# Products of the identity in TensorE's three waits ahead of the first FFN unit

## The chip, the cores and the metric

The kernel runs on one core of a Trainium2 chip. The metric is the device time of one execution in microseconds (us). TensorE (PE in the profile) multiplies, ScalarE (ACT) evaluates functions and copies, VectorE (DVE) does elementwise work and reductions, GpSimd (POOL) one elementwise step per pair of tiles, and SyncE (SP) issues the DMAs. Each engine takes its instructions in program order, and engines wait for each other by semaphores.

## The reference

Two stages. First, attention within chunks of 64 rows, for 8 batches, 8 heads, 576 rows and 64 columns per head:

```python
scores = scale * np.matmul(q_c, k_c.transpose(0, 1, 2, 4, 3))
attn = np.exp(scores - np.max(scores, axis=-1, keepdims=True))
attn = attn / (np.sum(attn, axis=-1, keepdims=True) + 1e-09)
out = np.matmul(attn, v_c)
```

Its output, laid out as 4608 tokens by 512, then goes through a feed-forward block with weights of 512 x 2048 and 2048 x 512:

```python
h = x @ w_in
g = h * (1.0 / (1.0 + np.exp(-1.702 * h)))
return (g @ w_out).astype(np.float32)
```

The weights arrive as 8-byte floats, which the kernel turns into pairs of 4-byte ones itself.

## The kernel before

The 4608 tokens are 36 tiles of 128, in 9 groups of 4. For each group the FFN is done in 16 units; unit j holds 128 columns of `w_in` and the matching 128 rows of `w_out`. Every large product is made of three products of fp32r parts (high by low, high by high, low by high), lines 634 to 636 for h, lines 669 to 671 for the output; the very first unit does h in two halves of 256 tokens (lines 647 to 649), the second of which needs tiles 2 and 3.

The first four tiles have code of their own, `plan_first(u)` for u = 0 to 3. For one tile: transposes of q and k (`t_pe`, L266), copies, scores (`s_pe`, L289), maximum and subtraction (DVE, L294 and L295), exponential (ACT, L298), sum and reciprocal (DVE, L302 to L305), normalisation (POOL, L308), transposes of the probabilities (`e_pe`, L313, tile eTp), their copy (`e_act`, ACT, L320), the product with v (`x_pe`, L329, tile x), and the split of its result in a high part (`x_hi`, ACT, L339) and a low part (`x_lo`, DVE, L342). The transposes of probabilities go to PSUM bank po2 for even u and po3 for odd u.

Over the same microseconds ACT and DVE convert the weights, `plan_w(j)`: ACT L172 and L176, DVE L181 and L182, DVE L188 (join), ACT L193 (high part of the unit's weights), DVE L196 (low part). FFN unit j needs both parts. After h of a unit, ACT applies the function and copies the high part (L655, L656), DVE makes the low part (L660, tile g_l), and only then may L669 begin.

The order of instructions on every engine is written once by `Plan.emit`: each step has an engine, a cost, a rank and what it needs, and a list scheduler with these costs picks the order. What a step's function emits has no influence on that order; only the step's cost and rank have.

Ahead of everything stands a warm-up: 7 products of the 128 x 128 fp32 identity with itself, in PSUM bank po3, planned at 3.4 us.

Of the kernel before, what the change touches and what calls it, by code (L numbers as in the profile page):

```python
# [9 lines left out]
F32 = mybir.dt.float32  # L10
# [8 lines left out]
PE, ACT, DVE, POOL, DMA = "pe", "act", "dve", "pool", "dma"  # L19
# [79 lines left out]
def tile_chunk_attention_ffn(  # L99
# [9 lines left out]
    nc = tc.nc  # L109
# [4 lines left out]
    P = 128  # L114
# [11 lines left out]
    WARM = 7  # L126
# [5 lines left out]
    ps_o = ctx.enter_context(tc.tile_pool(name="ps_o", bufs=1, space=bass.MemoryType.PSUM))  # L132
# [3 lines left out]
    ident = const.tile([P, P], F32, tag="ident", name="ident")  # L136
# [6 lines left out]
    plan = Plan(buffers)  # L143
# [9 lines left out]
    def plan_w(j):  # L153
# [58 lines left out]
        plan.add(ACT, 1.05, rank - 3.5, part_h, need=[e("wj")], make=e("wh"))  # L212
        plan.add(DVE, 1.25, rank - 2, part_l, need=[e("wh")], make=e("w"), give=["tmp"])


    x_h, x_l = {}, {}

# [23 lines left out]
    def plan_first(u):  # L241
# [68 lines left out]
        def e_pe():  # L310
            st["ps"] = ps = ps_o.tile([P, NP, 2, CH], F32, tag=f"po{2 + u % 2}", name=f"eTp_{u}")
            for n in range(NP):
                nc.tensor.transpose(  # L313
                    ps[:, n].rearrange("p h i -> p (h i)"),
                    st["e"][:, n].rearrange("p c j -> p (c j)"),
                    ident,
                )

        def e_act():
            nc.scalar.activation(st["et"], st["ps"], AF.Copy)  # L320

        def x_pe():
            va, et = st["v"], st["et"]
            ps = ps_a.tile([P, 2, 2, NP, CH], F32, tag="att", name=f"x_{u}")
            for n in range(NP):
                for h in range(2):
                    for c in range(2):
                        r = slice(64 * c, 64 * c + 64)
                        nc.tensor.matmul(  # L329
                            ps[64 * h : 64 * h + 64, c, 0, n, :],  # L330
                            va[r, 2 * n + h, :],
                            et[r, n, h, :],
                            start=True,
                            stop=True,
                        )
            st["x"] = ps[:, :, 0].rearrange("p c n i -> p n c i")

        def x_hi():
            nc.scalar.activation(x_part(x_h, u), st["x"], AF.Copy)  # L339

        def x_lo():
# [14 lines left out]
        plan.add(DVE, 1.1, rank + 0.6, s_sum, need=[ev("ex")], make=ev("z"))  # L356
        plan.add(POOL, 1.07, rank + 0.6, s_norm, need=[ev("z")], make=ev("n"))
        plan.add(PE, 0.5, rank + 1.7, e_pe, need=[ev("n")], make=ev("ep"), take=[f"po{2 + u % 2}"])
        plan.add(ACT, 0.6, rank + 1.7, e_act, need=[ev("ep")], make=ev("et"), give=[f"po{2 + u % 2}"])
        plan.add(  # L360
            PE, 0.75, rank + 1.5, x_pe, need=[ev("et"), ev("v"), "xa_0"], make=ev("xp"),
            take=["att", "att"], give=[slot(1)],
        )
# [354 lines left out]
                    make=f"st_{n}_{t}", give=[tag],  # L718
                )

    def warm_up():

        ps = ps_o.tile([P, P], F32, tag="po3", name="warm")
        for _ in range(WARM):
            nc.tensor.matmul(ps, ident, ident, start=True, stop=True)

    plan.add(PE, 3.4, -1000, warm_up)
    for u in range(TB):
        plan_first(u)
    for u in range(TB, NTL, 2):  # L730
# [41 lines left out]
```

## Time and profile before

| | us |
|---|---|
| median of 3 runs | 868.29 |
| lowest, highest | 868.08, 869.13 |
| the profiled execution | 868.24 |
| its span, first to last instruction | 866.5 |
| time outside the span (868.24 - 866.5) | 1.7 |
| PE busy | 849.3 |
| DVE busy | 392.3 |
| ACT busy | 319.1 |

The page gives averages over a long steady stretch, some 820 us, in which TensorE works without a pause. The part around the change is the ramp ahead of it, between about 21 and 41 us from the span's start, and is to be read from views cut to that stretch: the order of time on single engines, the busy time of short windows, and the chain that ended last. Start times in the order of time are relative to the span's start. TensorE's rows have a record for each pass that the profiler saw, and one matmul instruction of the program may leave more than one record: the 7 products of the warm-up are 14 records.

### The profile page before, as it was taken

Reading aid. Unit: us, or ns where it says so; the run is one execution under the profiler, and the core shown is the slowest. Engines: PE = TensorE matmul, PEld = TensorE weight load, DVE = VectorE, ACT = ScalarE, POOL = GpSimd, SP = SyncE. Lnnn points to the kernel's source line nnn. Section 1 sums busy time; section 2 is a strip of 40 time slices with the busy share of each in tenths; the row PEclk is TensorE's granted clock in tenths of the full one; section 3 lists DMA queues with packets and bytes.
Section 4 is the critical chain, followed back from the end, with each engine's and each line's share of the span. In section 5 each row is a group of like instructions: output and inputs, shape, how many; then the busy total and the mean of one; then the engine's idle time right before and its main releaser. Section 6 shows DMA issues by size and latency. Waiting matters only on the chain.

```text
span 866.5 us, 14153 instructions
## 1 busy us (share of the span) xinstructions
PE 849.3 (98%) x5882; PEld 703.0 (81%) x5882; DVE 392.3 (45%) x511; ACT 319.1 (37%) x459; POOL 32.3 (4%) x24
## 2 busy tenths in 40 slices
PE   7699999999999999999999999999999999999998
PEld 5588888888888888888888888888888888888886
DVE  5899985353534252616253444445343524121111
ACT  3999652332424242324242423223241424222221
POOL 1000000000000000000000000000000000000000
PEclk9799999999999999999999999999999999999999
DMA  9997243234313022402231232113101010010001
GB/s 236 319 300 212 45 74 80 52 56 73 92 25 49 22 47 57 72 2 48 74 58 18 41 75 51 31 38 85 25 1 26 37 35 3 1 45 5 1 0 49
DMA packets 194592, 55.47 MB, mean 64 GB/s; under 512 B 179680, under 2 KB 187872, under 8 KB 194528
## 3 DMA queue, kind: packets, MB, share of 16 engines
q1 hardware_dynamic: 194528, 54.57, 27.3%
q8 instruction: 46, 0.75, 0.4%
q14 instruction: 18, 0.15, 0.1%
HBM read 45.09 MB, written 9.44 MB: 63 GB/s over the span
## 4 chain that ended last, share of the span: by engine, by line
PE 95%; SPq 2%; DMA 1%; DVE 1%; ACT 1%; issue 1%; POOL 0%; DVEq 0%; POOLq 0%; ACTq 0%
PE po L669 16%; PE po L670 15%; PE po L671 15%; PE hp L634 15%; PE hp L635 15%; PE hp L636 15%; PE s L445 2%; PE x L510 2%; SPq L231 1%; DMA raw<-in_moe_w_out_dram 1%; PE qkTp L412 0%; ACT raw L172 0%; POOL first_b L308 0%; PE eTp L480 0%; SPq L163 0%
## 5 line engine op out<-in xcount | busy, mean ns | idle before, releaser
L660 DVE TENSOR_TENSOR g_l<-hp,g_h 128x512 fp32r<-128x512 f32 x144 | 99.5, 691 | 351.2 <-ACT g_h L656 350.1
L669 PE MATMUL po<-w,g_l 128*128 128x512 f32 x576 | 226.4, 393 | 0.1
L671 PE MATMUL po<-w,g_h 128*128 128x512 f32 x576 | 224.3, 389 | 0.0
L670 PE MATMUL po<-w,g_h 128*128 128x512 f32 x576 | 224.2, 389 | 0.0
L634 PE MATMUL hp<-x_l,w 128*128 128x512 f32 x572 | 223.2, 390 | 0.0
L636 PE MATMUL hp<-x_h,w 128*128 128x512 f32 x572 | 222.7, 389 | 0.0
L635 PE MATMUL hp<-x_h,w 128*128 128x512 f32 x572 | 222.6, 389 | 0.0
L655 ACT ACTIVATE hp<-hp 128x512 f32<-128x512 f32 x144 | 83.9, 583 | 305.3 <-PE hp L636 269.6
L656 ACT ACTIVATE g_h<-hp 128x512 fp32r<-128x512 f32 x144 | 86.1, 598 | 141.3 <-PE po L671 139.6
L669 PEld LDWEIGHTS po<-w,g_l 128*128 128x128 f32 x576 | 108.1, 188 | 23.9 <-DVE g_l L660 1.0
L671 PEld LDWEIGHTS po<-w,g_h 128*128 128x128 f32 x576 | 108.1, 188 | 22.7
L670 PEld LDWEIGHTS po<-w,g_h 128*128 128x128 f32 x576 | 108.1, 188 | 21.8
L636 PEld LDWEIGHTS hp<-x_h,w 128*128 128x128 f32 x572 | 107.4, 188 | 22.8 <-DVE w L196 0.4
L634 PEld LDWEIGHTS hp<-x_l,w 128*128 128x128 f32 x572 | 107.4, 188 | 22.4 <-DVE g_l L660 0.2
L635 PEld LDWEIGHTS hp<-x_h,w 128*128 128x128 f32 x572 | 107.4, 188 | 22.0
L493 DVE STREAM_TRANSPOSE eT<-e 32x512 f32<-32x512 f32 x112 | 78.7, 703 | 29.6 <-POOL e L473 27.8
L473 POOL TENSOR_TENSOR e<-e,r 128x1024 f32<-128x1024 f32 x14 | 26.7, 1905 | 671.8 <-ACT hp L655 671.8
L427 DVE STREAM_TRANSPOSE qkT<-raw 128x1024 f32<-128x1024 f32 x28 | 34.7, 1240 | 29.4 <-PE s L445 26.8
L525 ACT ACTIVATE x_h<-x 128x512 fp32r<-128x512 f32 x32 | 17.4, 593 | 58.4 <-PE x L510 58.4
L466 DVE TENSOR_REDUCE z<-e 128x16 f32<-128x1024 f32 x16 | 19.5, 1219 | 22.2 <-ACT e L462 22.2
L528 DVE TENSOR_TENSOR x_l<-x,x_h 128x512 fp32r<-128x512 f32 x32 | 20.6, 685 | 6.7 <-ACT x_h L525 6.7
L445 PEld LDWEIGHTS s<-qkT 64*64 64x64 f32 x1024 | 18.2, 135 | 5.6 <-issue 5.3
(64 smaller groups left out, 410.5 us busy)
## 6 DMA issues: line engine op xcount, KB each, us to landing
out_dram<-ob SPq DMA_DIRECT2D x36, 256.0 KB, 2.0
raw<-in_moe_w_in_dram SPq DMA_DIRECT2D x16, 512.0 KB, 7.8
raw<-in_moe_w_out_dram SPq DMA_DIRECT2D x16, 512.0 KB, 8.3
v<-in_v_dram SPq DMA_DIRECT2D x28, 256.0 KB, 3.3
raw<-in_q_dram SPq DMA_DIRECT2D x144, 32.0 KB, 2.0
raw<-in_k_dram SPq DMA_DIRECT2D x144, 32.0 KB, 2.0
raw<-in_q_dram SPq DMA_DIRECT2D x48, 24.0 KB, 1.9
raw<-in_k_dram SPq DMA_DIRECT2D x48, 24.0 KB, 1.9
```

What stands on the lines that cost most here:

```text
L427: nc.vector.transpose(st["tr"][:, i].rearrange("p n (t j) -> p (n t) j", j=32), st["raw"][:, i].rearrange("p n t j -> p (n t) j"),)
L445: nc.tensor.matmul(o, tr[r, 0, n, cols], tr[r, 1, n, cols], start=True, stop=True)
L493: nc.vector.transpose(st["et"][po : po + 32, :, 32 * a : 32 * a + 32], st["e"][pi : pi + 32, :, 32 * b : 32 * b + 32],)
L634: nc.tensor.matmul(hp, wh, xl, start=cc == 0, stop=False)
L635: nc.tensor.matmul(hp, wh, xh, start=False, stop=False)
L636: nc.tensor.matmul(hp, wl, xh, start=False, stop=cc == NCC - 1)
L655: nc.scalar.activation(h_t[g], h_t[g], AF.Gelu_apprx_sigmoid)
L656: nc.scalar.activation(gh, h_t[g], AF.Copy)
L660: nc.vector.tensor_tensor(gl, h_t.pop(g), gh.bitcast(F32), op=ALU.subtract)
L669: nc.tensor.matmul(po, gl[:, c], w[:, 0, :], start=j == 0, stop=False)
L670: nc.tensor.matmul(po, gh[:, c], w[:, 0, :], start=False, stop=False)
L671: nc.tensor.matmul(po, gh[:, c], w[:, 1, :], start=False, stop=j == NF - 1)
```

## The change

The warm-up's function becomes `keep_warm(count, bank)`, and it is called at three more places, inside steps that exist: 36 products into po3 right behind the transposes of tile 2's probabilities, 15 into po3 right behind tile 2's product with v, and 4 into po2 right behind the transposes of tile 3's probabilities. No result of these products is read. Costs and ranks of the steps stay as they were, also of the two steps that grew.

```diff
+    def keep_warm(count, bank):
+
+        ps = ps_o.tile([P, P], F32, tag=bank, name="warm")
+        for _ in range(count):
+            nc.tensor.matmul(ps, ident, ident, start=True, stop=True)
+
...
                     st["e"][:, n].rearrange("p c j -> p (c j)"),
                     ident,
                 )
+            if u == 2:
+                keep_warm(36, "po3")
+            if u == 3:
+                keep_warm(4, "po2")
...
             st["x"] = ps[:, :, 0].rearrange("p c n i -> p n c i")
+            if u == 2:
+                keep_warm(15, "po3")
...
-    def warm_up():
-
-        ps = ps_o.tile([P, P], F32, tag="po3", name="warm")
-        for _ in range(WARM):
-            nc.tensor.matmul(ps, ident, ident, start=True, stop=True)
-
-    plan.add(PE, 3.4, -1000, warm_up)
+    plan.add(PE, 3.4, -1000, lambda: keep_warm(WARM, "po3"))
```

TensorE's order before, from tile 2's transposes of probabilities to the first FFN unit. Numbers in names only tell buffers apart: eTp_320 and x_340 belong to tile 2, eTp_364 and x_379 to tile 3, hp_401 is h of the first unit.

```order
L313 MATMUL eTp_320<-ident,first_b_150 128x128 x4
L329 MATMUL x_340<-first_b_150 64x64 x16
L313 MATMUL eTp_364<-ident,first_b_197 128x128 x4
L329 MATMUL x_379<-first_b_197 64x64 x16
L647 MATMUL hp_401<-x_l_81,w_369 128x256
```

The same place in the changed kernel, whose lines stand 6 to 12 further down. The x of tile 2 is now x_377, tile 3's transposes are eTp_417, its x is x_437.

```order
L319 MATMUL eTp_320<-ident,first_b_150 128x128 x4
L219 MATMUL warm<-ident 128x128 x36
L339 MATMUL x_377<-first_b_150 64x64 x16
L219 MATMUL warm<-ident 128x128 x15
L319 MATMUL eTp_417<-ident,first_b_197 128x128 x4
L219 MATMUL warm<-ident 128x128 x4
L339 MATMUL x_437<-first_b_197 64x64 x16
L659 MATMUL hp_459<-x_l_81,w_427 128x256
```

Nothing changed places; three runs of products were put in, each ahead of an instruction that waits for another engine. In the program tile 3's transposes now wait for TensorE's own 15 products too, whose bank po3 they write.

ScalarE's order over the same stretch, in the changed kernel: the high parts of tiles 2 and 3 (x_h) and the copy of tile 3's probabilities (first_b_197<-eTp_417) stand between steps of the weights' conversion.

```order
L172 ACTIVATE raw_245<-raw_245 128x1024
L351 ACTIVATE x_h_80<-x_377 128x4x128
L176 ACTIVATE raw_245<-raw_245 128x1024
L193 ACTIVATE w_427<-wtmp_365 128x1024
L330 ACTIVATE first_b_197<-eTp_417 128x512
L172 ACTIVATE raw_305<-raw_305 128x1024
L351 ACTIVATE x_h_80<-x_437 128x4x128
L176 ACTIVATE raw_305<-raw_305 128x1024
```

On ScalarE, VectorE, GpSimd and the DMA queue the order is the same as before, but for buffer numbers and line numbers.

## The prediction

> **What bounds the kernel now.** I began with the page's busy shares, went to short windows around the change, then to the chain that ended last, and last to the single engines in order of time. The page first:
>
> ```profile
> PE 849.3 (98%) x5882; PEld 703.0 (81%) x5882; DVE 392.3 (45%) x511; ACT 319.1 (37%) x459; POOL 32.3 (4%) x24
> PEclk9799999999999999999999999999999999999999
> ```
>
> TensorE is busy 98% of the span, and the granted clock falls in one slice near the start (the 7). Five windows show where:
>
> ```profile
> core 0: us, PE busy (x) PEld busy (x) DVE busy (x) ACT busy (x) POOL busy (x), PEclk, DMA share, GB/s
> 21.74:25.16 3.42, 0.00 (x0) 0.00 (x0) 1.27 (x2) 2.43 (x3) 0.00 (x0) 1.00 1.07 379
> 25.16:28.57 3.41, 1.13 (x32) 0.94 (x32) 3.27 (x7) 3.19 (x5) 1.50 (x1) 0.50 1.06 381
> 31.98:35.40 3.42, 3.42 (x16) 3.42 (x17) 3.38 (x4) 3.42 (x4) 0.00 (x0) 0.50 1.05 158
> 35.40:40.56 5.16, 5.03 (x31) 3.80 (x29) 4.91 (x7) 5.10 (x8) 0.00 (x0) 1.00 1.08 287
> ...
> 40.56:862.60 822.04, 822.04 (x5520) 680.03 (x5520) 363.63 (x469) 294.21 (x427) 26.67 (x14) 1.00 0.23 53
> ```
>
> TensorE does nothing for 3.42 us, then has half the clock from 25.16 to 35.40. From 40.56 to 862.60 it is never idle, and the view of its waits has no row after 41 us. So whatever the change does before 40.56 arrives at the end as it is: the time moves by as much as the first output product (L669 at 40.56) moves. And from 25 to 40.56 ACT and DVE are nearly full too (5.10 and 4.91 of 5.16 us in the fourth window). The chain of waits, in order of time, says who sets 40.56:
>
> ```profile
> 22.73 1.11 ACT raw L172
> 23.86 0.71 DVE wtmp L181
> ...
> 27.07 1.86 POOL first_b L308
> ...
> 34.70 0.95 ACT w L193
> ...
> 39.82 0.70 DVE g_l L660
> ...
> 40.56 0.50 PE po L669
> ```
>
> It goes through the weights' conversion on ACT and DVE; TensorE's small steps of tiles 2 and 3 hang between. So TensorE's half clock is paid mostly beside a queue that is full anyway, but a late TensorE step stops that queue, since ACT takes its instructions in order.
>
> **The cost of one fill product.** The trace has such products only in the warm-up, at half clock. TensorE's rows in order of time, and two sources:
>
> ```profile
> 1.36 3.35 PE L725 MATMUL warm<-ident 128*128 128x128 f32 x14 [1.36 <-POOL ident masks.py:199]
> ...
> 16.78 1.04 PE L266 MATMUL qkTp<-ident,first_a 128*128 128x128 f32 x8
> 17.75 0.69 PE L329 MATMUL x<-first_b 64*64 64x64 f32 x32
> ...
> 21.06 0.65 PE L313 MATMUL eTp<-ident,first_b 128*128 128x128 f32 x4 [1.22 <-POOL first_b L308]
> 25.91 1.13 PE L329 MATMUL x<-first_b 64*64 64x64 f32 x32 [4.19 <-ACT first_b L320]
> 28.97 1.12 PE L313 MATMUL eTp<-ident,first_b 128*128 128x128 f32 x4 [1.93 <-POOL first_b L308]
> 30.78 1.13 PE L329 MATMUL x<-first_b 64*64 64x64 f32 x32 [0.69 <-ACT first_b L320]
> ...
> 35.66 0.28 PE L647 MATMUL hp<-x_l,w 128*128 128x256 f32 x1
> 35.77 0.28 PE L648 MATMUL hp<-x_h,w 128*128 128x256 f32 x1
> ```
>
> ```profile
> L725 PE MATMUL warm<-ident x14: 421/421/579, 1.4 to 4.3; 128*128 128x128 f32 x14
> ```
>
> ```profile
> L266 PE MATMUL qkTp<-ident,first_a x32: 272/273/364, 4.5 to 17.5; 128*128 128x128 f32 x32
> ```
>
> Seven products are 14 records, so one product is two. The 14 take 3.35 us, the last 0.42 of it its own run through: (3.35 - 0.42) / 13 = 0.225 us apart with the slower first one, 0.213 in the middle. The windows show no lower clock that early, but the pace is that of half clock: in the window 31.98:35.40 the 16 records are 3.42 / 16 = 0.214 apart too, and a transpose of the same shape is 273 ns long at full clock (L266) where a fill record is 421. At full clock 8 such transposes stand (1.04 - 0.27) / 7 = 0.110, more exactly 0.109 us apart. I take 0.109 us a record, 0.218 a product. Bounds: exactly half of the 0.213, 0.1065; and some 0.118 of the records of L647 to L649 at full clock (0.11 between the two rows at 35.66 and 35.77, and the six before 36.37 the same within rounding), which are those of the 0.214 at half clock. The transposes are nearer, being fp32 with the identity as operand.
>
> So 36 products take 72 x 0.109 = 7.85 us, 15 take 3.27, 4 take 0.87. The three waits they stand in (the brackets) are 4.19, 1.93 and 0.69 us. **None fits.**
>
> [...]
>
> **The sum, step by step.** ACT and DVE rows that are moved:
>
> ```profile
> 25.76 1.12 ACT L172 ACTIVATE raw<-raw 128x1024 f32<-128x1024 f32 x1
> 27.11 0.60 ACT L339 ACTIVATE x_h<-x 128x512 fp32r<-128x512 f32 x1 [0.22 <-PE x L329]
> 27.60 1.14 ACT L176 ACTIVATE raw<-raw 128x1024 int32<-128x1024 uint32 x1
> 28.62 1.05 ACT L193 ACTIVATE w<-wtmp 128x1024 fp32r<-128x1024 f32 x1
> 30.13 0.60 ACT L320 ACTIVATE first_b<-eTp 128x512 f32<-128x512 f32 x1 [0.45 <-PE eTp L313]
> 30.62 1.16 ACT L172 ACTIVATE raw<-raw 128x1024 f32<-128x1024 f32 x1
> 31.98 0.60 ACT L339 ACTIVATE x_h<-x 128x512 fp32r<-128x512 f32 x1 [0.20 <-PE x L329]
> ...
> 34.59 1.05 ACT L193 ACTIVATE w<-wtmp 128x1024 fp32r<-128x1024 f32 x1
> ...
> 38.01 0.58 ACT L655 ACTIVATE hp<-hp 128x512 f32<-128x512 f32 x1
> ```
>
> ```profile
> 27.93 0.68 DVE L342 TENSOR_TENSOR x_l<-x,x_h 128x512 fp32r<-128x512 f32 x1
> ...
> 32.91 0.68 DVE L342 TENSOR_TENSOR x_l<-x,x_h 128x512 fp32r<-128x512 f32 x1
> ...
> 34.23 1.23 DVE L182 SCALAR_TENSOR_TENSOR wtmp<-raw,wtmp 128x1024 int32<-128x1024 int32 x1
> 35.67 1.23 DVE L196 TENSOR_TENSOR w<-wtmp,w 128x1024 fp32r<-128x1024 f32 x1 [0.21 <-ACT w L193]
> ...
> 39.82 0.68 DVE L660 TENSOR_TENSOR g_l<-hp,g_h 128x512 fp32r<-128x512 f32 x1
> ```
>
> 1. First fill. Tile 2's transposes give way at 21.06 + 0.65 - 0.27 + 0.11 = 21.55. The fill ends at 21.55 + 7.85 = 29.40. Its clock stays full, since the window that was empty is now full. Tile 2's x starts at 29.40 instead of 25.91.
> 2. At full clock x takes 0.69, so it ends at 30.09; ACT's x_h follows after 0.07 (27.11 against 25.91 + 1.13) at 30.17, was 27.11. Behind it on ACT stand L176 (0.49 later) and the first unit's L193 (1.02 after that): 31.68 to 32.73. DVE waits for x_h: x_l at 30.81, was 27.93.
> 3. Second fill. It starts when x's last record is out, 29.92, and its last slot ends at 33.19. Tile 3's transposes write its bank and wait for its last record to be through, 33.19 - 0.11 + 0.27 = 33.35, and 0.06 of handover: 33.41, was 28.97. POOL, which released them before, is long done.
> 4. They take 0.65: 34.07. ACT's L320 starts at 34.11, was 30.13, and ends at 34.71.
> 5. Third fill: from 33.41 + 0.65 - 0.27 + 0.11 = 33.90 to 34.77, against L320's end and 0.05: 34.76. Its 4 products cost 0.01. Tile 3's x runs from 34.77 to 35.46, so x_h could start at 35.53.
> 6. But ACT has L172 in between, at 34.11 + 0.49 = 34.60, and an ACT instruction starts some 0.09 before the one ahead ends: 34.60 + 1.16 - 0.09 = 35.67, was 31.98. **ACT is 3.69 us late**, and has no wait after it: the second unit's L193 starts at 38.28 and ends at 39.33, the first function (L655) at 41.70, was 38.01.
> 7. DVE's x_l of tile 3 is at 35.67 + 0.64 = 36.31 (was 32.91, so DVE has caught up some 0.3), L182 at 37.63 ends at 38.86, and L196 waits for ACT's 39.33 as it did before: 39.36, 3.69 late. From there DVE's rows close up as before and g_l is 3.69 late, at 43.51; L669 at 44.25. TensorE itself isn't later: h of the first unit needs x_l of tile 3 (36.99), and at full clock its last 12 records of 0.118 end near 38.5; the second unit then waits for its weights, 39.36 + 1.23 = 40.59, again 3.69 late.
>
> The sum: 868.24 + 3.69 = 871.93 for the profiled execution; the median of the runs is 0.05 above it, so 872.0. What the full clock gives is in it already (0.44 in each x, 0.47 in the transposes, 16 records of h times 0.095): it only shortens the wait behind the fills. By the bounds of a record the same steps give +3.4 (0.1065) and +4.6 (0.118), so 871.7 to 872.9. Weights' DMAs aren't moved ahead of the stop, and late users only find them landed.
>
> **The rivals.**
>
> A, the fills fit. If one product takes 0.109 and not 0.218, 36 take 3.92 and 15 take 1.64, and all three waits hold them. Then TensorE is at full clock and late nowhere; ACT's three waits for it (0.22, 0.45, 0.20) shrink, but DVE is full from 23.86 on and had only one wait for ACT, 0.21 us. The gain is 0.21: 868.1, no change that can be told. For it: the waits divided by the counts give 4.19 / 36 = 0.116 and 1.93 / 15 = 0.129, close to one record. Against it: the 14 records of 7 products. 8 in 100.
>
> B, the half clock is what sets the end, and the fills fit. Then the saved 0.44 + 0.47 + 0.44 + 16 x 0.095 = 2.87 us would all come out: 868.29 - 2.87 = 865.4, a gain of 0.33%. Against it: the ACT and DVE rows of the window 35.40:40.56. [...] 4 in 100.
>
> C, the first overrun counts and the others vanish beside it: without the second fill, tile 3's transposes would start at 29.92, L320 behind L193 at 32.65, and the same steps give x_h at 34.21 and +2.2 to +2.4, so 870.6. For it: each later wait is shorter because ACT is late. Against it: step 3, the second fill stands after x in TensorE's own order. 5 in 100.
>
> D, the fill doesn't hold the clock, and products run at 0.427: 36 are 15.4 us, tile 2's x starts at 36.9, some 11 late, and the time is 879 or more. Against it: the warm-up, the same products, brought the full clock (transposes 0.109 apart right after). 3 in 100.
>
> **How the numbers follow.** The forecast as worked out has 80 in 100, the rivals 8, 4, 5 and 3. The time is that of the forecast, 872.0. Its own range is 871.7 to 872.9 by the price of a record; handovers of 0.05 taken six times and the 0.2 to 0.8 us between runs of one kernel widen it to 870.6 to 873.3, which takes in C's upper part and holds 8 in 10. A difference of 0.2% (1.7 us) is about what a measurement tells from none: faster by more is B, 0.04; within it A, 0.08; slower C, D and the forecast, 0.88.
>
> **What would show it.** The changed profile should have 72, 30 and 8 records of warm, 0.109 us apart, granted clock 1.00 throughout from 5 us; tile 2's x near 29.4, tile 3's transposes near 33.4, TensorE idle little before them; ACT's x_h rows waiting for PE about 3 us; the first L669 near 44.25; and nothing different after it but that shift. If tile 2's x starts near 25.9, step 1 is wrong and A or B holds; if x starts at 29.4 but L669 moves by less than 2 us, the queue behind ACT had slack that I don't see; if the stretch from L669 to the end changes its length, the claim that the shift passes through is wrong.

## The result and the profile after

The changed kernel takes 872.97 us (median of 6 runs, 872.56 to 873.18), the kernel before 868.29 (6 runs, 868.08 to 869.13): a ratio of 1.0053, with an interval of 1.0042 to 1.0064. It is slower by 4.7 us. The forecast was 872.0, with 870.6 to 873.3.

The profiled execution took 873.18 us with a span of 871.4. Its page has TensorE busier and the dent in the clock gone:

```profile
PE 859.5 (99%) x5992; PEld 713.4 (82%) x5992; DVE 392.3 (45%) x511; ACT 319.3 (37%) x459; POOL 32.4 (4%) x24
PEclk9999999999999999999999999999999999999999
```

Both look like progress, and the kernel is slower: 10.2 us more busy time of TensorE and the full clock, for 4.7 us more. TensorE's rows of the changed kernel in order of time (start, length, instruction, records, and in brackets the wait ahead):

```profile
21.65 0.66 PE L319 MATMUL eTp<-ident,first_b 128*128 128x128 f32 x4 [1.22 <-POOL first_b L314]
22.14 8.20 PE L219 MATMUL warm<-ident 128*128 128x128 f32 x72
30.27 0.69 PE L339 MATMUL x<-first_b 64*64 64x64 f32 x32
30.90 3.62 PE L219 MATMUL warm<-ident 128*128 128x128 f32 x30
34.66 0.63 PE L319 MATMUL eTp<-ident,first_b 128*128 128x128 f32 x4
35.13 1.06 PE L219 MATMUL warm<-ident 128*128 128x128 f32 x8
...
45.44 0.50 PE L681 MATMUL po<-w,g_l 128*128 128x512 f32 x1 [0.16 <-DVE g_l L672]
```

There are 72, 30 and 8 records for 36, 15 and 4 products: two for each. The three waits of 4.19, 1.93 and 0.69 us ahead of tile 2's x, tile 3's transposes and tile 3's x have gone. Tile 2's x starts at 30.27 instead of 25.91, though its operand is ready at 26.2, as ScalarE's rows show (L330 at 25.59, 0.59 long). Now ScalarE waits for TensorE:

```profile
25.59 0.59 ACT L330 ACTIVATE first_b<-eTp 128x512 f32<-128x512 f32 x1
...
31.04 0.60 ACT L351 ACTIVATE x_h<-x 128x512 fp32r<-128x512 f32 x1 [3.83 <-PE x L339]
...
35.33 0.60 ACT L330 ACTIVATE first_b<-eTp 128x512 f32<-128x512 f32 x1 [1.71 <-PE eTp L319]
...
36.88 0.60 ACT L351 ACTIVATE x_h<-x 128x512 fp32r<-128x512 f32 x1
...
39.45 1.07 ACT L193 ACTIVATE w<-wtmp 128x1024 fp32r<-128x1024 f32 x1
```

The brackets were 0.22 and 0.45 before; they are 3.83 and 1.71 now. The second x_h has no bracket: L172 ahead of it ends last, as step 6 said. VectorE's low part of the second unit's weights waits for that L193, as it did before, and the low part of g comes 4.88 later:

```profile
40.55 1.23 DVE L196 TENSOR_TENSOR w<-wtmp,w 128x1024 fp32r<-128x1024 f32 x1 [0.49 <-ACT w L193]
...
44.70 0.68 DVE L672 TENSOR_TENSOR g_l<-hp,g_h 128x512 fp32r<-128x512 f32 x1
```

The first output product moves from 40.56 to 45.44, by 4.88. After it nothing changes: the window from there to the last product is 822.00 us of busy TensorE, where it was 822.04.

```profile
45.50:867.50 822.00, 822.00 (x5520) 679.95 (x5520) 363.69 (x469) 294.35 (x427) 26.69 (x14) 1.00 0.23 51
```

So all of the loss arises between 21 and 45 us. In the chain that ended last, the fills now stand as links, where the wait for the weights' DMA stood:

```profile
22.30 8.04 PE warm L219 x72
30.34 0.62 PE x L339 x32
30.97 3.56 PE warm L219 x30
```

### The profile page after: what moved, and what is told of

Read it like the earlier page. It is cut to its first block, busy times and chain, and to the rows that moved or that the text cites. A ratio compares the mean times of both kernels' runs of the same rounds, so it can differ in the third digit from the quotient of the medians.

```text
span 871.4 us, 14374 instructions
## 1 busy us (share of the span) xinstructions
PE 859.5 (99%) x5992; PEld 713.4 (82%) x5992; DVE 392.3 (45%) x511; ACT 319.3 (37%) x459; POOL 32.4 (4%) x24
## 4 chain that ended last, share of the span: by engine, by line
PE 97%; DVE 1%; ACT 1%; issue 1%; POOL 0%; POOLq 0%; DVEq 0%; ACTq 0%
PE po L681 15%; PE po L683 15%; PE po L682 15%; PE hp L646 15%; PE hp L647 15%; PE hp L648 15%; PE s L457 2%; PE x L522 2%; PE warm L219 2%; PE qkTp L424 0%; PE s L295 0%; ACT raw L172 0%; POOL first_b L314 0%; PE eTp L319 0%; PE qkTp L272 0%
## 5 line engine op out<-in xcount | busy, mean ns | idle before, releaser
L439 DVE STREAM_TRANSPOSE qkT<-raw 128x1024 f32<-128x1024 f32 x28 | 34.7, 1240 | 29.4 <-PE s L457 26.8
```

What stands on the lines that cost most here:

```text
L439: nc.vector.transpose(st["tr"][:, i].rearrange("p n (t j) -> p (n t) j", j=32), st["raw"][:, i].rearrange("p n t j -> p (n t) j"),)
```

## The experiments

Seven kernels, each timed against the kernel before on the same chip. All start from the changed kernel, and the order on ScalarE, VectorE, GpSimd and the DMA queue is the same in each of them. The theory is that of the prediction: a product is two records, the fills overrun their waits, ScalarE stands still meanwhile, and its delay arrives at the end. The main rivals: that the fills' presence and not their length hurts, and that the half clock is worth something by itself.

**Fills that fit.** The counts are cut to 17, 6 and 2.

```diff
-                keep_warm(36, "po3")
+                keep_warm(17, "po3")
-                keep_warm(4, "po2")
+                keep_warm(2, "po2")
-                keep_warm(15, "po3")
+                keep_warm(6, "po3")
```

> The three fills are cut to 17, 6 and 2 products, so that at two records of 0.112 us each (3.8, 1.3 and 0.45 us) they end before the waits they stand in do. Theory of the prediction (the loss is the overrun; the ramp is bound by ScalarE and VectorE): the clock stays full, tile 2's x starts near 26, tile 3's transposes near 29, the first output product near 40.35 (was 40.56), and the time is 0.2 us below the kernel before, 868.1, not to be told from it. Rival B (the half clock set the end): 2.9 us less than before, 865.4. A rival by which fills themselves hurt, whatever their length: 1 us or more above before.

Measured: 868.02 us (867.11 to 868.72, 11 runs) against 868.18 (22 runs), ratio 0.9996 (0.9987 to 1.0005). TensorE in order of time:

```profile
21.53 3.96 PE L219 MATMUL warm<-ident 128*128 128x128 f32 x34
25.51 0.69 PE L339 MATMUL x<-first_b 64*64 64x64 f32 x32
26.14 1.60 PE L219 MATMUL warm<-ident 128*128 128x128 f32 x12
28.52 0.66 PE L319 MATMUL eTp<-ident,first_b 128*128 128x128 f32 x4 [0.78 <-POOL first_b L314]
29.02 0.61 PE L219 MATMUL warm<-ident 128*128 128x128 f32 x4
30.02 0.69 PE L339 MATMUL x<-first_b 64*64 64x64 f32 x32 [0.39 <-ACT first_b L330]
```

The fills end before what they wait for, every step runs at full clock (0.69 and 0.66 in place of 1.13 and 1.12), and between 20 and 47 us ScalarE has no wait for TensorE left. The time is that of before. Rival B, which asked for 2.9 us, is out. The gain is there, but small: from the first weights' conversion (the first L172, which waits 3.15 us for their DMA here) to the first output product it is 17.58 us, against 17.83 before. These 0.25 us stand against the 0.21 of rival A's sum. The kernel before had the half clock for 10.24 us (25.16 to 35.40). To have the full clock there was worth 0.25, since another queue set the end of that stretch.

Still, TensorE's steps at half clock did not all run beside that queue: in the chain of the kernel before, two of them are links.

```profile
28.97 1.13 PE eTp L313 x4
...
30.78 1.18 PE x L329 x32
```

The full clock shortens these two by 0.47 and 0.44 us. But VectorE had waited only 0.21 us for ScalarE at the end of this chain (L196). When the chain got shorter, VectorE ended last, and there the gain stopped: in this run the trace shows no wait of VectorE from 24.14 us to the first output product.

**The same counts, shorter instructions.** Each of the 55 products becomes a transpose of the identity: same operands, same bank, same place.

```diff
         for _ in range(count):
-            nc.tensor.matmul(ps, ident, ident, start=True, stop=True)
+            if count == WARM:
+                nc.tensor.matmul(ps, ident, ident, start=True, stop=True)
+            else:
+                nc.tensor.transpose(ps, ident, ident)
```

> All three fills with the counts of the change, but each product replaced by a transpose of the identity (same operands and shape), which should leave one record of 0.109 to 0.112 us. Theory (the loss is two records per product): 36 take 4.0, 15 take 1.7, 4 take 0.45 us, all fit; tile 2's x near 25.9 to 26.3; time 868.1 to 868.4, as before. If the number of instructions or their place hurts, and not their length: 872 to 873. On the clock: if transposes count as work it stays full as in the change; if they don't, it falls to half near 25 as before.

Measured: 868.31 us (867.52 to 868.85, 11 runs) against 868.18, ratio 1.0001 (0.9993 to 1.0010).

```profile
22.05 4.09 PE L222 MATMUL warm<-ident 128*128 128x128 f32 x36
26.08 0.69 PE L342 MATMUL x<-first_b 64*64 64x64 f32 x32
26.70 1.86 PE L222 MATMUL warm<-ident 128*128 128x128 f32 x15
28.71 0.63 PE L322 MATMUL eTp<-ident,first_b 128*128 128x128 f32 x4
```

36 instructions leave 36 records and 4.09 us, where they left 72 and 8.20. This gives rival A its condition, one record per instruction, and the whole loss is gone. What hurts is neither the place of the fills nor their count, but the time that the second record of each product adds.

**The first fill alone.** The 15 and the 4 are taken out.

```diff
-            if u == 3:
-                keep_warm(4, "po2")
-            if u == 2:
-                keep_warm(15, "po3")
```

> Only the first fill (36 products), the others taken out. Theory: tile 2's x near 29.6 to 30.3, tile 3's transposes right behind it, ScalarE's copy of them behind the weights' high part, first output product 2.6 to 3.2 us later than before; time 871.1 (870.8 to 871.6). If the first overrun accounts for the whole loss (rival C): as the change, 872.6 to 873.2.

Measured: 871.54 us (871.25 to 872.55, 5 runs) against 868.18, ratio 1.0041 (1.0029 to 1.0054), 3.4 us more.

```profile
22.58 0.66 PE L319 MATMUL eTp<-ident,first_b 128*128 128x128 f32 x4 [1.22 <-POOL first_b L314]
23.07 8.20 PE L219 MATMUL warm<-ident 128*128 128x128 f32 x72
31.21 0.69 PE L337 MATMUL x<-first_b 64*64 64x64 f32 x32
31.83 0.66 PE L319 MATMUL eTp<-ident,first_b 128*128 128x128 f32 x4
```

The time is at the upper end of what was expected (870.8 to 871.6), and above the 2.2 to 2.4 us that rival C's sum gave the first fill alone. Rival C held that the first overrun is all of it; it isn't. From tile 2's transposes to the first output product this kernel takes 22.25 us and the changed one 23.79, so the second and third fill cost 1.5 us on top. This profiled execution, at 872.55 the slowest of its five, shows something else: tile 2's transposes start at 22.58, 1.5 later than before, since the full clock came only at 10.91 us (the scores at 7.49 still took 1.98 us, in the changed kernel those at 7.39 took 1.15). With that, the first output product comes 4.27 us later than before (44.83), where 2.6 to 3.2 were expected; without the 1.52 ahead of the first fill it is 2.75. The five runs lie in two groups, 871.25 to 871.54 and 872.40 to 872.55, but when the full clock began is on record for the profiled one alone.

**The second and third fill alone.** The 36 are taken out.

```diff
-            if u == 2:
-                keep_warm(36, "po3")
```

> Only the second and third fill (15 and 4 products), the first taken out, so TensorE is idle 4 us as before and the clock falls. Theory with records of 0.213 us until a whole window has been busy: the second fill ends near 32.7, tile 3's transposes start near 33, the end is some 3.2 us later: 871.5 (870.8 to 872.2), though the overrun at full clock would be only 1.2 us. If the records kept their full-clock price: 0.5 us later, 868.8. If losses of the fills simply add up to the change's 4.7: 4.7 less what the first alone costs, about 2.0, so 870.3.

Measured: 871.01 us (870.83 to 871.63, 6 runs) against 868.18, ratio 1.0033 (1.0021 to 1.0045), 2.8 us more. This is inside the expected 870.8 to 872.2 and above the 870.3 of losses that add up. The two parts alone cost 3.4 and 2.8, together 6.2, and the whole change only 4.7. The row of the second fill says why, with the clock in the windows below it:

```profile
25.89 1.13 PE L337 MATMUL x<-first_b 64*64 64x64 f32 x32 [3.67 <-ACT first_b L328]
26.96 5.55 PE L219 MATMUL warm<-ident 128*128 128x128 f32 x30
32.65 0.63 PE L319 MATMUL eTp<-ident,first_b 128*128 128x128 f32 x4
```

```profile
20.80:24.22 3.42, 0.66 (x4) 0.42 (x4) 1.74 (x4) 1.51 (x2) 0.71 (x1) 1.00 1.03 367
24.22:27.63 3.41, 1.74 (x35) 1.62 (x36) 3.24 (x6) 2.49 (x4) 0.58 (x1) 0.50 1.03 381
27.63:31.05 3.42, 3.42 (x18) 3.42 (x18) 2.94 (x5) 2.74 (x4) 1.27 (x1) 0.50 1.08 383
```

Without the first fill the clock falls at 24.22, and the same 30 records take 5.55 us in place of 3.62; it comes back at 31.05, behind a stretch that was busy throughout. These 1.93 us are more than the 1.5 between 6.2 and 4.7. The 36 that overrun also pay for a cheaper second fill.

**A delay ahead, with and without the change.** Ten products right behind the scores of tile 3, ahead of tile 2's transposes: once with none of the three fills, once with all.

```diff
                         nc.tensor.matmul(sc[r, n, c, :], t[r, 0, n, cols], t[r, 1, n, cols], start=True, stop=True)
+            if u == 3:
+                keep_warm(10, "po3")
```

> None of the change's fills; instead 10 products of the identity right behind the scores of tile 3, ahead of tile 2's transposes of probabilities, where TensorE waits 1.2 us. They take 20 x 0.112 = 2.2 us, so these transposes come about 1.0 us later. Theory (before the change this stretch waits for the first unit's weights by DMA, landed near 22.7, and ScalarE's copy isn't due before 25.3): the second is hidden, first output product and time as before, 868.2, within 0.3. Rival (TensorE's early work sets the time in any kernel): 1.0 above, 869.2.

> The changed kernel with the same 10 products behind tile 3's scores. Theory (with the fills TensorE's own order sets the time from the first transposes on, so that anything ahead of the first fill passes to the end): first output product and time 1.0 us later than the change, 873.9 (873.5 to 874.4). If the wait for the weights' DMA still covered it: 873.0 as the change.

Measured without the fills: 868.36 us (867.88 to 868.94, 11 runs) against 868.28 (16 runs), ratio 1.0003 (0.9994 to 1.0012). With them: 873.86 (873.39 to 874.02, 5 runs), ratio 1.0065 (1.0052 to 1.0077), 0.9 us above the change's 872.97. TensorE without the fills, then with them:

```profile
19.70 2.50 PE L219 MATMUL warm<-ident 128*128 128x128 f32 x20
22.04 0.60 PE L321 MATMUL eTp<-ident,first_b 128*128 128x128 f32 x4
26.06 1.13 PE L337 MATMUL x<-first_b 64*64 64x64 f32 x32 [3.42 <-ACT first_b L328]
```

```profile
20.07 2.50 PE L219 MATMUL warm<-ident 128*128 128x128 f32 x20
22.41 0.60 PE L321 MATMUL eTp<-ident,first_b 128*128 128x128 f32 x4
22.84 8.20 PE L219 MATMUL warm<-ident 128*128 128x128 f32 x72
30.98 0.69 PE L341 MATMUL x<-first_b 64*64 64x64 f32 x32
```

In the first the transposes are 1 us late (22.04 against 21.06) and only the bracket of x shrinks (3.42 against 4.19). In the second x starts as late as the fill ends. So the wait that the change fills was also a reserve: TensorE's early work could be 1 us late and the time didn't show it.

**A shorter first fill.** 26 products in place of 36, the other two as in the change.

```diff
-                keep_warm(36, "po3")
+                keep_warm(26, "po3")
```

> The change with 26 products in the first fill in place of 36, the others as they are. Theory (the loss is the overrun, product by product): 10 x 2 x 0.112 = 2.23 us less than the change, 870.7 (870.3 to 871.2). If a fill of that length only had to be there to block ScalarE, whatever its length: 872 to 873.

Measured: 870.76 us (870.13 to 871.38, 6 runs) against 868.28, ratio 1.0031 (1.0019 to 1.0042): 2.2 us below the change, for 20 records that are 0.112 apart (2.24). The first fill is now 5.97 us long (8.20 in the change), and tile 2's x starts at 27.79. From tile 2's transposes to the first output product it is 21.55 us (42.94 - 21.39), 2.24 less than the change's 23.79:

```profile
21.89 5.97 PE L219 MATMUL warm<-ident 128*128 128x128 f32 x52
```

Side by side, the starts in each profiled execution in us, and the two distances that tell the kernels apart:

| kernel | tile 2's transposes | first L172 | first output product | from first L172 | from tile 2's transposes |
|---|---|---|---|---|---|
| before | 21.06 | 22.73 | 40.56 | 17.83 | 19.50 |
| without fills, ten ahead | 22.04 | 22.87 | 40.73 | 17.86 | 18.70 |
| 17, 6, 2 | 21.04 | 22.23 | 39.81 | 17.58 | 18.77 |
| transposes | 21.56 | 22.22 | 39.81 | 17.59 | 18.25 |
| the change | 21.65 | 22.97 | 45.44 | 22.47 | 23.79 |
| the change, ten ahead | 22.41 | 22.99 | 46.15 | 23.16 | 23.74 |

In the first four kernels the end hangs on the landing of the first weights: the distance from L172 stays within 0.28 us, while that from the transposes varies by 1.25. In the last two it hangs on TensorE: the distance from the transposes is the same within 0.05, that from L172 is not. The two kernels whose fills fit had their weights 0.5 us earlier in the profiled execution than the kernel before. Their medians don't show such a gain, and why the weights landed earlier there isn't settled.

## Why the prediction was right, point by point

**Direction and mechanism were right.** A product is two records, as read from the 14 records of the warm-up. None of the fills fits; ScalarE stands still ahead of the x_h of tile 2 (3.83 us); L172 and not x ends last before the second x_h (step 6); VectorE's L196 passes the delay on (step 7); and the 822 us behind it don't change. The signs that were named came, but later at each step: tile 2's x at 30.27 for 29.4, tile 3's transposes at 34.66 for 33.4, the first output product at 45.44 for 44.25.

**The size was 1.2 us short in the profiled execution (4.88 in place of 3.69), 1.0 in the median.** The measured 872.97 lies just above the 871.7 to 872.9 that the price of a record gave, and inside the forecast range only because that was widened for handovers and for the spread between runs. Three terms of the sum:

- Step 1, the start of the first fill, the largest: taken as 21.55 from the execution of before, it was 22.14, 0.59 later. The full clock came at 6.98 us in place of 4.68: the first transposes of q and k, at 4.51 and 4.50, took 2.01 us in place of 1.43, and tile 2's transposes came at 21.65 in place of 21.06. The sum treated this start as given. It varies from execution to execution, and the changed kernel has given up the reserve that hid it.
- The price of a record: 0.109 was taken from transposes, and the fills' records are 0.112 apart, between the bounds of 0.1065 and 0.118. For 102 records of the first two fills that is 0.27 us. The transposes experiment has its records 0.109 apart, so the row was the right one for a transpose and a little low for a product.
- Handovers: from the first fill to x 0.09, ahead of the second fill 0.11, its first record (0.38 long, where the median is 0.28) 0.10, and from its last record to tile 3's transposes 0.15 in place of 0.06. Together some 0.4, where the sum had most of them at nothing.

These are 0.59 + 0.27 + 0.39 = 1.25; 0.06 came back on the way to the first output product. This division holds for the profiled execution; how late the other runs reached full clock isn't on record.

**Step 2 and the clock.** The clock stayed full through the fills, as forecast (1.00 from 21.70 to 35.20), and what it gives was rightly put at nearly nothing: 0.25 us where the fills fit (experiment), against 0.21 in the sum of rival A.

**The rivals.** A fell on the record count, and the transposes show that its sum was right for its condition. B fell with the fills that fit. C fell with the first fill alone: the other two cost 1.5 us on top. D fell on the granted clock of 1.00: a product of the fills took two records 0.112 apart, 0.224, where it had 0.427.

**Not forecast:** that the second fill would cost more without the first (expected only after the result, and found), and that the time ahead of the first fill would come to count. The prediction also had TensorE's half clock paid mostly beside the queue of ScalarE and VectorE, and its excerpt of the chain leaves out that two of TensorE's steps at half clock are links. That cost the forecast nothing: rival A's sum had found the real bound, VectorE's one wait of 0.21 us.

## What to carry to other kernels

Filling waits with more work than they held turned them into links of the chain here (8.04 and 3.56 us of fills, 4.7 us in the time), while 17, 6 and 2 products fitted and left it as it was (868.02): price each filler in records of the trace, at the clock that it will run at, and leave a margin. Before paying for a clock, look whether the engine that gets it ends last in that stretch: here VectorE ended within 0.21 us of TensorE's chain, and the full clock through 10 us was worth 0.25. And the idle wait hid variation of what ran before: TensorE 1 us late left the time at 868.36 with the wait open, and with the wait filled the same ten products cost 0.9 us on top of the overrun.

## What the runs showed of the hardware beside that

**The granted clock in these executions.** In the kernel before the granted clock changed at 4.68, 25.16 and 35.40 us, 20.48 and 10.24 apart; in the first fill alone at 10.91, 34.80 and 38.21, 23.89 and 3.41 apart. In the changed kernel full clock began at 6.98. The windows below are as long as the shortest of these distances. The changed kernel up to its rise, then the first fill alone, ahead of its late rise (columns: stretch, its length, busy time of PE first):

```profile
3.57:6.98 3.41, 2.95 (x14) 2.32 (x12) 0.43 (x1) 0.60 (x1) 0.00 (x0) 1.00 1.27 223
```

```profile
0.67:4.08 3.41, 2.72 (x12) 2.72 (x13) 0.00 (x0) 1.28 (x1) 0.50 (x2) 1.00 0.67 148
4.08:7.49 3.41, 2.54 (x11) 1.83 (x11) 0.69 (x1) 0.60 (x1) 0.00 (x0) 1.00 1.29 220
```

After 2.95 us of work the clock rose; after 2.72 and 2.54 it didn't. (These windows say 1.00 because there is no record of the clock before its first change; the last four records of the warm-up, which take 1.06 us in the first fill alone, 0.213 apart, say half.) Downwards, in the first fill alone, in the kernel with ten products ahead and no fills, and in the kernel before:

```profile
31.39:34.80 3.41, 1.10 (x36) 0.79 (x32) 2.17 (x3) 2.83 (x4) 0.00 (x0) 1.00 1.25 201
34.80:38.21 3.41, 3.14 (x41) 3.02 (x42) 3.41 (x5) 3.23 (x5) 0.00 (x0) 0.50 0.81 231
```

```profile
21.34:24.75 3.41, 1.29 (x12) 1.05 (x10) 1.00 (x3) 1.88 (x2) 0.00 (x0) 1.00 1.08 379
24.75:28.17 3.42, 1.13 (x32) 0.94 (x32) 3.28 (x6) 3.21 (x6) 0.96 (x1) 0.50 1.06 379
```

```profile
18.33:21.74 3.41, 1.92 (x44) 1.46 (x36) 3.12 (x7) 0.78 (x2) 1.04 (x1) 1.00 1.07 372
```

It fell after stretches with 1.10 and 1.29 us of work, and held after one with 1.92. So in these traces it fell also after stretches that weren't empty. These are single executions, and no run shows that busy time alone decides it.

**Transposes held the clock.** In the experiment with transposes the stretch from 20.65 to 24.06 has nothing but transposes on TensorE, 2.50 us of them, and the granted clock is 1.00 in the next:

```profile
20.65:24.06 3.41, 2.50 (x23) 2.50 (x24) 2.16 (x4) 1.84 (x2) 0.85 (x1) 1.00 1.04 373
24.06:27.48 3.42, 3.42 (x59) 3.19 (x57) 3.25 (x6) 3.09 (x6) 0.86 (x1) 1.00 1.05 376
```

So here fp32 transposes of 128 x 128 held the full clock, where it fell after the stretches with 1.29 and 1.10 us of work above. Whether transposes alone would also raise it, no run shows.
